# Attention and top-1 experts on one core: six products behind the next branch, an alignment directive for small products, and a new order at the first border

## The chip, the cores and the metric

The kernel runs on one core of a Trainium2 chip. The metric is the device time of one execution in microseconds (us); the time shown is the median of three runs. Durations come from one execution taken by the hardware profiler.

## The reference

Attention inside blocks of 64 rows, then a mixture of eight experts of which each row uses the best one. Everything is float32.

```python
# q, k, v: (8, 8, 576, 64); chunks of 64 rows
scores = scale * q_c @ k_c.T
attn = softmax(scores)
x = (attn @ v_c) -> (4608, 512)
logits = x @ w_gate                     # (4608, 8)
expert = argmax(logits); gate = softmax(logits)[expert]
for e in range(8):
    xe = x[expert == e]
    h = maximum(xe @ w1[e], 0.0)        # w1: (512, 1024)
    out[expert == e] = gate * (h @ w2[e])   # w2: (1024, 512)
```

## The kernel before, in words

Matrix products of float32 accuracy are made as three fp32r products: each operand is split into a high part and the rest (`whi`, `wlo`; `xhi`, `xlo`; `hh`, `hl`), and high by high, high by low and low by high are summed in PSUM. Each such product is a weight load and a matmul on TensorE.

The first 165 us compute the attention in 18 groups, the gate logits and the routing, and scatter the rows of x, sorted by expert, to a table `xd` in DRAM. Slot 0 of the expert stage is woven into it: `slot_0` is a generator whose steps `filler(n)` takes one by one. Its last three steps are: three products of m=0 and three of m=1 of its last hidden block (two steps), then `finish` for both (the last step).

The expert stage is a loop over slots. A slot is 256 rows of one expert (`BLK`), two row tiles of 128, and up to 128 extra rows (`EXT`), so that an expert's remainder needs no slot of its own. How many extra rows there are is known only at run time, so every slot's code holds three forms, chosen by `kind{u}`: `form_a` (256 rows), `form_x(64)` (320 wide) and `form_x(128)` (384 wide). In TensorE's program the 128-row form of a slot stands first, then the 64-row form, then the plain one, then the code behind the join, called the merge here. With the given data 18 slots are run; slots 1, 5 and 7 take the 64-row form, slot 11 the 128-row form, the others the plain one. Slots from 14 on (`SMIN`) stand inside a further condition.

What a slot does, with the lines before the change:
- `make_xt` (L572, L574, L575): transposes of the row tiles on TensorE into PSUM, a copy to `xhi` on ScalarE, the rest `xlo` on VectorE. Slots 0 to 2 use it. Later slots get their rows turned by `spread` (16 transfers on SP's queue), `turn` (VectorE) and `make_xs`. `make_xt_x` (L605, L607, L608) does the same as `make_xt` for the extra rows, in every slot.
- `gemm1` (L616) or `gemm1_x` (L623, L624's sum): for f = 0 to 7 twelve products into one PSUM bank; ScalarE makes `hh` (L637), VectorE `hl` (L642).
- `block(f)`: `gemm2` (L694 to L696), three products of 512 columns for m=0 (bank U) and three for m=1 (bank V). `more(f)`: `gemm2_x` for the extra rows (bank K).
- `finish(u, m)`: scales a result by the gate (L715 to L721) and scatters it to the output (L722, on POOL).

In the forms `block(f-2)` runs behind `gemm1(f)`, so the loop ends with blocks 6 and 7 open; their hidden tiles (`last`, from pool `hq`, reused by every slot) are used in the merge: both m=0 parts, `finish` 0, both m=1 parts, `finish` 1. That the order is kept comes from `manual_schedule`: each engine gets its instructions in the order in which the code is written.

At each slot's f=4 a hint is given to TensorE on the branch of the next slot. TensorE's code is fetched in blocks by DMA, on a queue named "q8 instruction". `fill_up` (L1164) puts tiny products of 8 columns into the 64- and 128-row forms, with counts from `FILL`: slot 1 has 12 behind f=4 of the 64-row form; slots from 2 on have 10 at the head of the 128-row form, and 16 at the head and 23 behind f=4 of the 64-row form. Their results are never read.

Of the kernel before, what the change touches and what calls it, by code (L numbers as in the profile page):

```python
# [18 lines left out]
P = 128  # L19
# [13 lines left out]
BLK = 256  # L33
# [5 lines left out]
XW = D + 16  # L39
HB = 3  # L40
WARM = 36
FILL = {1: (0, 0, 12), 2: (10, 16, 23)}
BIG = 1.0e6


# [1 line left out]
def attn_moe_kernel(ctx: ExitStack, tc: tile.TileContext, q, k, v, wg, w, out):  # L47
# [479 lines left out]
    def wset(u):  # L527

        return 0 if u < 2 else (u + 1) % 2
# [115 lines left out]
    def gemm1(par, f, hh=None, hl=None):  # L645
        ph = bank("X", [P, BLK]) if f % 3 == 2 else bank("S", [P, BLK])
        gemm1_pe(par, f, ph)
        return gemm1_lo(ph, relu_hi(ph, hh), hl)
# [32 lines left out]
    def filler(n):  # L681
        for _ in range(n):
            next(fill, None)
            halves[0] -= 1
# [425 lines left out]
    hx = ctx.enter_context(tc.tile_pool(name="hx", bufs=HB))  # L1110
    hq = ctx.enter_context(tc.tile_pool(name="hq", bufs=1))
    filler(halves[0] - 2)
    make_xt(1, banks="QK")
    filler(3)
    def slot(u, kd, nxt):
        par = wset(u)
        py = [bank("UV"[m], [P, D]) for m in range(2)]
        if u > 1:
            spread(u + 1)
            load_w(u + 1, 2)  # L1120

        last = [[hq.tile([P, BLK], F32R, name=f"{x}{f}") for x in ("hh", "hl")] for f in (6, 7)]

        def block(f, h, ms=(0, 1)):
            for m in ms:
                gemm2(par, f, h, m, py)

        def later():

            if u == 1:  # L1130
                yield from places()
            yield from find_u(u + 3)

        def some(x, n):
            for _ in range(n):
                next(x, None)

        def form_a():
            h = []
            x = later()  # L1140
            for f in range(8):
                h.append(gemm1(par, f, *(last[f - 6] if f > 5 else ())))
                if f == 4 and u + 1 < SMAX:

                    tc.mark_branch_hint_location(f"kind{u + 1}", hint=(nxt + 1) >> 1, engines=PE)
                if f == 0 and u > 1:
                    gather_x(u + 1)
                if f == 5 and u > 1:
                    turn()
                    gather(u + 2)  # L1150
                if f < 7:
                    split_step(u, f)
                    some(x, 4 if u == 1 else 1)
                if f > 1:
                    block(f - 2, h[f - 2])

        def form_x(n):

            make_xt_x(u, n)
            pe = bank("K", [P, D])  # L1160

            def fill_up(to, k):
                for _ in range(k):
                    nc.tensor.matmul(to[:, 0:8], ones, ones[:, 0:8], start=True, stop=True)  # L1164

            few = FILL[min(u, 2)]
            fill_up(pe, few[0] if n == EXT else few[1])
            h = []
            x = later()

            def more(f):
                gemm2_x(par, f, *h[f][1], pe)

            for f in range(8):
                h.append(gemm1_x(par, f, n, *(last[f - 6] if f > 5 else ())))
                if f == 4 and u + 1 < SMAX:
                    tc.mark_branch_hint_location(f"kind{u + 1}", hint=(nxt + 1) >> 1, engines=PE)
                if f == 0 and u > 1:
                    gather_x(u + 1)
                if f == 5 and u > 1:  # L1180
                    turn()
                    gather(u + 2)
                if f < 7:
                    split_step(u, f)
                    some(x, 4 if u == 1 else 1)
                if 1 < f < 7:
                    block(f - 2, h[f - 2][0])
                    more(f - 2)
                if f == 4 and n < EXT:
                    fill_up(bank("T", [P, P]), few[2])  # L1190
            more(5)
            more(6)
            block(5, h[5][0], (0,))
            more(7)
            finish(u, 2, pe, n)
            block(5, h[5][0], (1,))

        with tc.If(kd > 0, label=f"kind{u}") as c:
            with tc.If(kd > 1) as c2:
                form_x(EXT)  # L1200
            with c2.Else():
                form_x(EXT // 2)
        with c.Else():
            form_a()

        nc.gpsimd.drain()  # L1206
        if u == 1:
            make_xt(u + 1)
        else:
            make_xs()  # L1210
        split_chunk(wset(u + 1), 5)
        for m in range(2):
            for f in (6, 7):
                block(f, last[f - 6], (m,))
            finish(u, m, py[m], on_act=m == 0)

    n_s = nc.values_load(kind[0:1, NU:NU + 1], min_val=0, max_val=SMAX)
    PE = [mybir.EngineType.PE]
    kinds = {1: nc.values_load(kind[0:1, 1:2], min_val=0, max_val=2)}
    nest = ExitStack()  # L1220
    for u in range(1, SMAX):
        if u >= SMIN:
            nest.enter_context(tc.If(n_s > u))
        kd = kinds[u]
        if u + 1 < SMAX:
            kinds[u + 1] = nc.values_load(kind[0:1, u + 1:u + 2], min_val=0, max_val=2)
        slot(u, kd, kinds.get(u + 1))
    nest.close()
    order.__exit__(None, None, None)

# [33 lines left out]
```

## Time and profile before

| | |
|---|---|
| median of three runs | 606.31 us (605.6 to 609.58) |
| the profiled execution | 606.66 us, span 604.5 us |
| mean granted TensorE clock | 0.981 |
| TensorE matmul busy | 566.5 us, 94% of the span |
| TensorE weight load busy | 496.8 us, 82% |
| VectorE busy | 443.5 us, 73% |
| ScalarE busy | 300.9 us, 50% |
| GpSimd (POOL) busy | 265.0 us, 44% |

The span runs from the first to the last instruction; the profiled execution is some 2 us longer. The times inside the trace count from the span's start. A product is listed with the time it is busy (0.39 us for 512 columns), but products are pipelined: from the start of one to the start of the next 0.23 us pass. A number in brackets at the end of a row is the idle time of the engine ahead of it, and what ended it; "issue" is time in which the engine waited for nothing that the profile shows. An engine name with a q (PEldq) is its sequencer, which reads the program, waits for semaphores, and takes branches.

### The profile page before, as it was taken

How to read it: one execution, taken by the hardware profiler on the slowest of the kernel's cores; microseconds unless marked ns; L12 is line 12 of the kernel's file. 1: busy time of each engine (PE TensorE's matmuls, PEld its weight loads, DVE VectorE, ACT ScalarE, POOL GpSimd, SP SyncE). 2: the span in 40 equal slices, each digit the busy share in tenths (PEclk: the TensorE clock that was granted, in tenths of full speed). 3: DMA queues.
4: the chain of work that ended last, by engine and by line, in shares of the span. 5: the costliest groups of instructions: out<-in, count | busy, mean ns of one | idle time of the engine just before them, and what ended most of it. 6: DMA issues, size and time to landing. Idle time of an engine off the chain costs nothing.

```text
span 604.5 us, 14989 instructions
## 1 busy us (share of the span) xinstructions
PE 566.5 (94%) x5723; PEld 496.8 (82%) x5723; DVE 443.5 (73%) x834; ACT 300.9 (50%) x563; POOL 265.0 (44%) x275
## 2 busy tenths in 40 slices
PE   7887879779989999999999999999998999999995
PEld 5666767658878989988898888998897899899894
DVE  6687969885747677876677668788655878878774
ACT  2565556664123555554455355555434555555552
POOL 3122424474645255435264436525423453654352
PEclk9898989898989999999999999999999999999999
DMA  8999898632485364256226612358622235632021
GB/s 296 367 354 348 289 333 292 220 110 108 163 286 199 123 219 111 79 176 226 58 68 216 219 43 84 109 197 299 218 87 84 60 108 176 216 96 85 20 57 37
DMA packets 59701, 103.31 MB, mean 171 GB/s; under 512 B 16240, under 2 KB 32624, under 8 KB 55984
## 3 DMA queue, kind: packets, MB, share of 16 engines
q0 software_dynamic: 20704, 60.74, 29.5%
q1 hardware_dynamic: 38864, 40.94, 21.1%
q8 instruction: 67, 1.10, 0.8%
q14 instruction: 66, 0.54, 0.3%
HBM read 121.60 MB, written 19.82 MB: 234 GB/s over the span
## 4 chain that ended last, share of the span: by engine, by line
PE 59%; DMA 19%; issue 8%; POOL 4%; DVE 4%; POOLq 3%; ACT 2%; SPq 0%; ACTq 0%; DVEq 0%
DMA out_y<-y,oid 15%; PE psS L616 11%; PE psS L623 6%; PE psL L616 3%; PE psU L696 3%; PE psV L694 3%; PE psV L695 3%; PE psU L694 3%; PE psU L695 3%; PE psV L696 3%; PE psU L286 3%; PE psS L232 3%; POOLq L1206 2%; PE psL L623 2%; POOL raw L532 2%
## 5 line engine op out<-in xcount | busy, mean ns | idle before, releaser
L77 DVE TENSOR_TENSOR wlo<-raw,whi 128x1024 fp32r<-128x1024 f32 x134 | 163.3, 1219 | 27.0 <-ACT whi L76 24.2
L76 ACT CAST whi<-raw 128x1024 fp32r<-128x1024 f32 x134 | 139.9, 1044 | 0.5 <-issue 0.5
L532 POOL DMA_INDIRECT raw<-in_w,widx x70 | 87.9, 1256 | 108.3 <-DVE wlo L77 50.7
L637 ACT ACTIVATE hh<-psS 128x256 fp32r<-128x256 f32 x110 | 42.3, 385 | 167.2 <-PE psS L616 113.7
L616 PE MATMUL psS<-xlo,whi 128*128 128x256 f32 x344 | 97.5, 283 | 2.3 <-DVE xlo L575 2.3
L616 PE MATMUL psS<-xhi,whi 128*128 128x256 f32 x344 | 97.7, 284 | 1.1 <-PE psV L696 0.9
L616 PE MATMUL psS<-xhi,wlo 128*128 128x256 f32 x344 | 97.3, 283 | 0.0
L722 POOL DMA_INDIRECT out_y<-y,oid x40 | 46.0, 1150 | 109.7 <-issue 27.3
L642 DVE SCALAR_TENSOR_TENSOR hl<-psS,hh 128x256 fp32r<-128x256 f32 x110 | 46.3, 421 | 56.5 <-ACT hh L637 33.3
L550 POOL DMA_INDIRECT xg<-xd,idx x58 | 68.0, 1173 | 21.8 <-issue 18.3
L616 PEld LDWEIGHTS psS<-xlo,whi 128*128 128x128 f32 x344 | 65.8, 191 | 5.2 <-DVE xlo L575 2.5
L616 PEld LDWEIGHTS psS<-xhi,whi 128*128 128x128 f32 x344 | 65.7, 191 | 5.2 <-issue 1.7
L616 PEld LDWEIGHTS psS<-xhi,wlo 128*128 128x128 f32 x344 | 65.7, 191 | 0.0
L694 PE MATMUL psU<-whi,hh 128*128 128x512 f32 x144 | 57.5, 399 | 1.6 <-issue 1.6
L695 PE MATMUL psU<-wlo,hh 128*128 128x512 f32 x144 | 57.1, 397 | 0.0
L694 PE MATMUL psV<-whi,hh 128*128 128x512 f32 x144 | 56.9, 395 | 0.0
L696 PE MATMUL psU<-whi,hl 128*128 128x512 f32 x144 | 56.6, 393 | 0.2
L695 PE MATMUL psV<-wlo,hh 128*128 128x512 f32 x144 | 56.7, 394 | 0.0
L696 PE MATMUL psV<-whi,hl 128*128 128x512 f32 x144 | 56.2, 391 | 0.0
L427 POOL DMA_INDIRECT xd<-xb,di x32 | 31.5, 985 | 33.4 <-issue 21.6
L84 POOL TENSOR_TENSOR wlo<-raw,whi 128x512 fp32r<-128x512 f32 x15 | 19.0, 1277 | 52.4 <-ACT whi L83 38.6
L594 DVE STREAM_TRANSPOSE y<-xg 128x1024 f32<-128x1024 f32 x16 | 33.1, 2069 | 0.9 <-issue 0.3
(247 smaller groups left out, 1192.9 us busy)
## 6 DMA issues: line engine op xcount, KB each, us to landing
kb<-in_k SPq DMA_DIRECT2D x36, 256.0 KB
qt<-in_q SPq DMA_DIRECT2D x36, 256.0 KB
vb<-in_v SPq DMA_DIRECT2D x36, 256.0 KB
xg<-xg SPq DMA_DIRECT2D x256, 32.0 KB
raw<-in_w SPq DMA_DIRECT2D x16, 256.0 KB
raw<-in_w,widx POOLq DMA_INDIRECT x70, 3.3
xg<-xd,idx POOLq DMA_INDIRECT x58, 3.6
out_y<-y,oid POOLq DMA_INDIRECT x40, 3.2
```

The source lines that it names most:

```text
L76: nc.scalar.copy(hi, src)
L77: nc.vector.tensor_tensor(lo, src, hi.bitcast(F32), ALU.subtract)
L532: nc.gpsimd.indirect_dma_start(out=raw[c][:, :], out_offset=None, in_=w, in_offset=bass.IndirectOffsetOnAxis(ap=widx[:, u, c:c + 1], axis= ...
L550: nc.gpsimd.indirect_dma_start(out=t[:, :], out_offset=None, in_=xd[0:rows, :], in_offset=bass.IndirectOffsetOnAxis(ap=place(u, h), axis=0 ...
L616: nc.tensor.matmul(ph, a, b[:, kc, 0:BLK], start=kc + i == 0, stop=kc + i == 5)
L623: nc.tensor.matmul(ph, a[par][kc][:, f * 128:(f + 1) * 128], b[:, kc, 0:BLK + n], start=kc + i == 0, stop=kc + i == 5)
L637: nc.scalar.activation(hh, ph, AF.Relu)
L642: nc.vector.scalar_tensor_tensor(hl, ph, 0.0, hh.bitcast(F32), ALU.max, ALU.subtract)
L694: nc.tensor.matmul(py, hh, wh, start=f == 0, stop=False)
L695: nc.tensor.matmul(py, hh, wl, start=False, stop=False)
L696: nc.tensor.matmul(py, hl, wh, start=False, stop=f == 7)
L722: nc.gpsimd.indirect_dma_start(out=outs[m], out_offset=bass.IndirectOffsetOnAxis(ap=oid[u % 3][0:n, m:m + 1], axis=0), in_=y, in_offset=No ...
```

## The change

The change does four things, all on TensorE's order or driven by it:

1. The tiny products go. In their place one `addr_align` directive stands behind f=4 of the 64-row form (not in the 128-row form).
2. In slots 1 to 12 the six m=1 products of blocks 6 and 7 and `finish` 1 (now called `rest`) move from the merge into the next slot's form: ahead of `gemm1` in the plain form, between the extra rows' transposes and `gemm1_x` in the others. In their place block 5, until now the last of the form, moves into the merge. In the x forms block 4 moves behind `more(5)`. From slot 13 on `rest` is run at once, and the merge keeps 18 products.
3. The hidden tiles are now a fixed list for all slots, as many as before.
4. Slot 0's last six products stand between the transposes of slot 1's two row tiles; its `finish` stands behind both.

```diff
-FILL = {1: (0, 0, 12), 2: (10, 16, 23)}
+PLACE = {1: 180, 2: 189}
+BLOCK = 256
...
     filler(halves[0] - 2)
-    make_xt(1, banks="QK")
-    filler(3)
-    def slot(u, kd, nxt):
+    make_xt(1, 0, banks="QK")
+    filler(2)
+    make_xt(1, 1, banks="QK")
+    filler(1)
+    h_of = h0[5:8] + h0[5:8] + [[hq.tile([P, BLK], F32R, name=f"{x}{f}") for x in ("hh", "hl")] for f in (6, 7)]
+
+    def rest(u, py):
+
+        for f in (6, 7):
+            gemm2(wset(u), f, h_of[f], 1, py)
+        finish(u, 1, py[1])
+
+    def slot(u, kd, nxt, left=None):
...
         def form_a():
+            if left is not None:
+                rest(u - 1, left)
             h = []
...
-                if f > 1:
+                if 1 < f < 7:
                     block(f - 2, h[f - 2])
...
             make_xt_x(u, n)
+            if left is not None:
+                rest(u - 1, left)
             pe = bank("K", [P, D])
 
-            def fill_up(to, k):
-                for _ in range(k):
-                    nc.tensor.matmul(to[:, 0:8], ones, ones[:, 0:8], start=True, stop=True)
-
-            few = FILL[min(u, 2)]
-            fill_up(pe, few[0] if n == EXT else few[1])
...
+                if 1 < f < 6:
+                    block(f - 2, h[f - 2][0])
                 if 1 < f < 7:
-                    block(f - 2, h[f - 2][0])
                     more(f - 2)
                 if f == 4 and n < EXT:
-                    fill_up(bank("T", [P, P]), few[2])
+                    nc.tensor.addr_align(BLOCK, offset=PLACE[min(u, 2)], max_nops=0)
             more(5)
+            block(4, h[4][0])
             more(6)
-            block(5, h[5][0], (0,))
             more(7)
             finish(u, 2, pe, n)
-            block(5, h[5][0], (1,))
...
         split_chunk(wset(u + 1), 5)
-        for m in range(2):
-            for f in (6, 7):
-                block(f, last[f - 6], (m,))
-            finish(u, m, py[m], on_act=m == 0)
+        block(5, h_of[5])
+        for f in (6, 7):
+            block(f, h_of[f], (0,))
+        finish(u, 0, py[0], on_act=True)
+        if u + 1 < SMIN:
+            return py
+        rest(u, py)
...
-        slot(u, kd, kinds.get(u + 1))
+        left = slot(u, kd, kinds.get(u + 1), left)
```

TensorE at the border of slots 0 and 1 (`xg_64` are slot 1's row tiles, psQ and psK their two banks, `kind` the register with the form). Before, both row tiles' transposes come first and the six products behind them:

```order
L696 MATMUL psV<-whi_7_75,hl 128x512
L572 MATMUL psQ<-ident,xg_64 128x128 x4
L572 MATMUL psK<-ident,xg_64 128x128 x4
L694 MATMUL psU<-whi_7_75,hh 128x512
L695 MATMUL psU<-wlo_7_83,hh 128x512
L696 MATMUL psU<-whi_7_75,hl 128x512
L694 MATMUL psV<-whi_7_75,hh 128x512
L695 MATMUL psV<-wlo_7_83,hh 128x512
L696 MATMUL psV<-whi_7_75,hl 128x512
L1217 TENSOR_LOAD kind
```

After it, the same place:

```order
L697 MATMUL psV<-whi_7_75,hl 128x512
L573 MATMUL psQ<-ident,xg_64 128x128 x4
L695 MATMUL psU<-whi_7_75,hh 128x512
L696 MATMUL psU<-wlo_7_83,hh 128x512
L697 MATMUL psU<-whi_7_75,hl 128x512
L695 MATMUL psV<-whi_7_75,hh 128x512
L696 MATMUL psV<-wlo_7_83,hh 128x512
L697 MATMUL psV<-whi_7_75,hl 128x512
L573 MATMUL psK<-ident,xg_64 128x128 x4
L1227 TENSOR_LOAD kind
```

The six products have passed the second group of transposes, and the loads of the form's register stand directly behind that group (line numbers are one or more higher in the changed kernel).

TensorE at the head of slot 2's 64-row form, which stands for that of every later slot (`xg_65` are the extra rows, `ones` the operand of the tiny products). Before:

```order
L695 MATMUL psV<-wlo_6_3053,hh 128x512
L696 MATMUL psV<-whi_6_3045,hl 128x512
L1199 UNCONDITIONAL_BRANCH
L605 MATMUL psT<-ident,xg_65 128x64 x4
L1164 LDWEIGHTS ones
L1164 MATMUL psK<-ones 128x8
```

After, from the same branch on:

```order
L1206 UNCONDITIONAL_BRANCH
L606 MATMUL psT<-ident,xg_65 128x64 x4
L695 MATMUL psV<-whi_7_75,hh_3110 128x512
L696 MATMUL psV<-wlo_7_83,hh_3110 128x512
L697 MATMUL psV<-whi_7_75,hl_3111 128x512
L695 MATMUL psV<-whi_7_75,hh_3112 128x512
L696 MATMUL psV<-wlo_7_83,hh_3112 128x512
L697 MATMUL psV<-whi_7_75,hl_3113 128x512
L624 MATMUL psS<-xhi,whi_0_3039 128x320
```

The tiny products have gone, and slot 1's last six products (its weights, `whi_7_75`) stand in their place.

TensorE at the end of slot 1's merge, up to slot 2's branch. Before:

```order
L696 MATMUL psU<-whi_7_75,hl_3155 128x512
L694 MATMUL psV<-whi_7_75,hh_3152 128x512
L695 MATMUL psV<-wlo_7_83,hh_3152 128x512
L696 MATMUL psV<-whi_7_75,hl_3153 128x512
L694 MATMUL psV<-whi_7_75,hh_3154 128x512
L695 MATMUL psV<-wlo_7_83,hh_3154 128x512
L696 MATMUL psV<-whi_7_75,hl_3155 128x512
L1226 TENSOR_LOAD kind
L1198 COMPARE_AND_BRANCH
L1199 COMPARE_AND_BRANCH
```

After:

```order
L697 MATMUL psV<-whi_6_74,hl 128x512
L695 MATMUL psU<-whi_7_75,hh_3110 128x512
L696 MATMUL psU<-wlo_7_83,hh_3110 128x512
L697 MATMUL psU<-whi_7_75,hl_3111 128x512
L695 MATMUL psU<-whi_7_75,hh_3112 128x512
L696 MATMUL psU<-wlo_7_83,hh_3112 128x512
L697 MATMUL psU<-whi_7_75,hl_3113 128x512
L1237 TENSOR_LOAD kind
L1205 COMPARE_AND_BRANCH
L1206 COMPARE_AND_BRANCH
```

The branch now stands directly behind the m=0 products, the m=1 products have gone behind it, and the products of block 5 (weights `whi_6_74`) stand ahead of the m=0 ones.

## Rows read from the trace of the kernel before

**Rows 1.** Windows: length, busy time of PE, PEld, DVE, ACT, POOL, then clock, DMA share, GB/s.
```profile
164.65:168.07 3.42, 1.50 (x8) 0.85 (x6) 0.11 (x1) 0.59 (x1) 2.81 (x3) 1.00 0.67 177
168.07:171.48 3.41, 3.34 (x10) 2.58 (x10) 2.19 (x7) 0.59 (x1) 1.00 (x2) 0.50 0.84 262
200.00:427.00 227.00, 226.32 (x1460) 203.49 (x1459) 169.45 (x295) 118.01 (x197) 104.52 (x84) 1.00 0.46 148
...
462.00:581.00 119.00, 119.00 (x770) 108.69 (x769) 92.07 (x148) 65.51 (x101) 58.55 (x50) 1.00 0.36 109
```

**Rows 2.** Timeline of PE, border of slots 0 and 1: start, length, instruction, [idle before].
```profile
166.56 0.75 PE L572 MATMUL psQ<-ident,xg 128*128 128x128 f32 x4 [1.15 <-DMA xg<-xd,idx]
168.14 1.13 PE L572 MATMUL psK<-ident,xg 128*128 128x128 f32 x4 [0.83 <-DMA xg<-xd,idx]
...
169.91 0.63 PE L696 MATMUL psU<-whi,hl 128*128 128x512 f32 x1
...
171.66 0.69 PE L605 MATMUL psT<-ident,xg 64*128 64x64 f32 x4
172.81 0.86 PE L623 MATMUL psS<-xhi,whi 128*128 128x320 f32 x4 [0.46 <-ACT xhi L607]
...
176.25 0.56 PE L623 MATMUL psS<-xhi,wlo 128*128 128x320 f32 x2 [0.53 <-issue]
...
177.22 0.60 PE L623 MATMUL psL<-xhi,whi 128*128 128x320 f32 x3
```

**Rows 3.** Timeline of PE, the head of slot 5, a 64-row slot.
```profile
272.14 0.55 PE L1164 MATMUL psK<-ones 128*128 128x8 bf16 x16
272.67 0.71 PE L623 MATMUL psS<-xhi,whi 128*128 128x320 f32 x3
```

**Rows 4.** Timeline of PE, slot 5 behind f=4.
```profile
287.10 0.73 PE L1164 MATMUL psT<-ones 128*128 128x8 bf16 x23
287.69 0.68 PE L623 MATMUL psL<-xhi,whi 128*128 128x320 f32 x3
```

**Rows 5.** Timeline of PE, the head of slot 11, the 128-row slot.
```profile
423.94 0.63 PE L605 MATMUL psT<-ident,xg 128*128 128x128 f32 x4
424.41 0.39 PE L1164 MATMUL psK<-ones 128*128 128x8 bf16 x10
425.30 0.62 PE L623 MATMUL psS<-xhi,whi 128*128 128x384 f32 x2 [0.50 <-ACT xhi L607]
```

**Rows 6.** Timeline of PE, the end of slot 5.
```profile
298.60 0.39 PE L710 MATMUL psK<-whi,xh 128*128 128x512 f32 x1
...
300.42 0.39 PE L695 MATMUL psU<-wlo,hh 128*128 128x512 f32 x1
300.89 0.50 PE L696 MATMUL psU<-whi,hl 128*128 128x512 f32 x1
```

**Rows 7.** Timelines of PEld and DVE, the same place.
```profile
300.89 0.19 PEld L696 LDWEIGHTS psU<-whi,hl 128*128 128x128 f32 x1 [0.51 <-DVE y L717]
...
300.36 0.48 DVE L717 TENSOR_SCALAR y<-y,gate 64x512 f32<-64x512 f32 x1
```

**Rows 8.** PE's sequencer by source line: durations min/median/max in ns, first and last start.
```profile
L1198 PEldq COMPARE_BRANCH  x17: 78/347/3254, 169.6 to 572.0; - x17
...
L1199 PEldq COMPARE_BRANCH  x8: 70/330/3680, 169.7 to 454.0; - x8
...
L1226 PEldq TENSOR_LOAD <-kind x17: 300/307/325, 169.2 to 571.5; - x17
```

**Rows 9.** DMA queues in the window 174.0 to 175.1 us: packets, MB, share.
```profile
q0 software_dynamic: 90, 0.39, 89.4%
q8 instruction: 1, 0.02, 5.6%
```

**Rows 10.** Timeline of PE, the end of slot 11.
```profile
455.80 0.39 PE L696 MATMUL psV<-whi,hl 128*128 128x512 f32 x1
457.79 0.50 PE L694 MATMUL psU<-whi,hh 128*128 128x512 f32 x1 [1.60 <-issue]
```

More of the change, by code (lines that the diff above doesn't have):

```diff
@@ L1120, in slot @@
             load_w(u + 1, 2)
-        last = [[hq.tile([P, BLK], F32R, name=f"{x}{f}") for x in ("hh", "hl")] for f in (6, 7)]
         def block(f, h, ms=(0, 1)):
@@ L1141, in form_a @@
             for f in range(8):
[L1142 to L1153, printed above, removed]
-                if f > 1:
[L1155 to L1160, printed above, removed]
-            def fill_up(to, k):
-                for _ in range(k):
-                    nc.tensor.matmul(to[:, 0:8], ones, ones[:, 0:8], start=True, stop=True)
-            few = FILL[min(u, 2)]
-            fill_up(pe, few[0] if n == EXT else few[1])
[L1168 to L1175, printed above, removed]
+                h.append(gemm1(par, f, *h_of[f]))
                 if f == 4 and u + 1 < SMAX:
@@ L1186, in form_x, with more @@
                 if 1 < f < 7:
+                    block(f - 2, h[f - 2])
+        def form_x(n):
+            make_xt_x(u, n)
+            if left is not None:
+                rest(u - 1, left)
+            pe = bank("K", [P, D])
+            h = []
+            x = later()
+            def more(f):
+                gemm2_x(par, f, *h[f][1], pe)
+            for f in range(8):
+                h.append(gemm1_x(par, f, n, *h_of[f]))
+                if f == 4 and u + 1 < SMAX:
+                    tc.mark_branch_hint_location(f"kind{u + 1}", hint=(nxt + 1) >> 1, engines=PE)
+                if f == 0 and u > 1:
+                    gather_x(u + 1)
+                if f == 5 and u > 1:
+                    turn()
+                    gather(u + 2)
+                if f < 7:
+                    split_step(u, f)
+                    some(x, 4 if u == 1 else 1)
+                if 1 < f < 6:
                     block(f - 2, h[f - 2][0])
+                if 1 < f < 7:
                     more(f - 2)
                 if f == 4 and n < EXT:
-                    fill_up(bank("T", [P, P]), few[2])
+                    nc.tensor.addr_align(BLOCK, offset=PLACE[min(u, 2)], max_nops=0)
             more(5)
+            block(4, h[4][0])
             more(6)
-            block(5, h[5][0], (0,))
             more(7)
             finish(u, 2, pe, n)
-            block(5, h[5][0], (1,))
         with tc.If(kd > 0, label=f"kind{u}") as c:
@@ L1220, in attn_moe_kernel @@
     nest = ExitStack()
+    left = None
     for u in range(1, SMAX):
```

## The prediction

> **What bounds the kernel now.** I read the windows view first, stage by stage. From 200 to 427 us TensorE is busy 226.32 of 227.00 us, from 462 to 581 us 119.00 of 119.00, both at full clock, while VectorE, the next but for TensorE's own weight loads, has 169 and 92 [rows 1]. So in the expert stage the end moves only by what TensorE is given to do and by the places where it stands still. The second view is TensorE's timeline at those places. At the border of slots 0 and 1 it has two holes, 1.15 and 0.83 us, both ended by a gather of rows; then it runs at half the clock (0.50, the 1.2 GHz level, for 3.41 us; of its six products the last four take 169.91 to 171.66, 0.44 each, where eight at full clock take 298.60 to 300.42, 0.23 each); then 0.46 us for ScalarE's xhi and 0.53 us that end in "issue" [rows 1, 2, 6]. At the head of a 64-row slot 16 tiny products stand ahead of the first gemm [rows 3], 23 more stand behind f=4 [rows 4], and the 128-row slot's head has 10 and then a wait of 0.50 us [rows 5]. At the end of a 64-row slot one weight load waits 0.51 us for VectorE's last step on the extra rows [rows 6, 7]. The sequencer's own rows (branches, register loads) come last: they price what the new order puts next to a branch [rows 8].
>
> **The change part by part.** The sum is made against the profiled execution, 606.66 us: the span of 604.5 and some 2 us around it, 0.35 above the median of 606.31. The shipped data takes the 64-row form in slots 1, 5 and 7, the 128-row form in slot 11, the plain form elsewhere; so of slots 2 to 12, in which six products now stand behind the branch, eight are plain.
>
> *Fillers gone.* Their cost is from start to start: at slot 5's head 272.14 to 272.67, 0.53 us [rows 3]; slot 7's head shows the same pattern, so 1.06 together. Behind f=4, 287.10 to 287.69, 0.59 us, twice 1.18, and slot 1's 12 at the same rate 12/23 of 0.59, 0.31 [rows 4]. The head fillers also gave ScalarE time to make xhi. In the new order the six products of the slot before (6 x 0.23 = 1.4 us) stand in that place. Slot 1, which has no head filler, needs 172.81 - 171.66 = 1.15 us from its transposes to the first gemm, 0.69 of it the transposes [rows 2]; 0.46 us are to be covered and 1.4 cover them. The six products themselves cost nothing new: they are done once before and once after. At slot 11's head both the fillers and the wait go: 424.41 to 425.30, 0.89 us [rows 5]. Bounds: all of it, or, if xhi were late all the same, the fillers alone and not the 0.50.
>
> *The directive.* No row of this trace shows an alignment directive. Below, the nearest row is a branch that falls through, 0.07 us on the sequencer [rows 8], hidden; above, a branch whose target is not there, 3.25 to 3.68 us. TensorE's queue holds work ahead of its sequencer: the first branch of the second kind runs at 169.7 and the first instruction behind it at 171.66 [rows 2, 8], so about 1.9 us of such a stall would be hidden and some 1.6 seen. I take 0, since of 17 and 8 branches the middle ones take 0.33 to 0.35 and lie under the products. Without the fillers the padding is the directive's work, so what stands behind it keeps its place in the blocks in which code is fetched.
>
> *Slot 1's start.* Row tile 1's transposes wait for their gather until 168.14, the six products do not [rows 2]. In the new order the products start when row tile 0's transposes end, about 167.0, at the full clock that this stretch has [rows 1], and end at 167.0 + 6 x 0.23 = 168.4; the transposes then take some 0.47 at full clock, as slot 11's four do [rows 5], to 168.9. The register loads and branches stay behind the transposes of row tile 1: the last load is at 169.2, the branches from 169.6 and 169.7 [rows 8], over at about 170.1. The extra rows' transposes then start near 170.3 instead of 171.66, and gemm1 near 171.5 instead of 172.81. That gain of 1.3 us runs into the hole at 176.25. There one block of code arrives on the instruction queue at about 175, through DMA engines that weights keep busy [rows 9], and nothing in the change makes it come earlier. But the 128-row form, which lies ahead of the 64-row one in TensorE's program, gives six products of block 5 to the merge, each a weight load and a matmul; the same block border therefore falls 12 instructions, or six products, later in slot 1's work: behind 24 products instead of 18. Six of them took 176.25 to 177.22, 0.16 each [rows 2]; 24 need 3.9 us, to 175.4, so f=2 begins at 176.25 instead of 177.22: -0.97. Bounds: 0, if the border stands where it did; -1.9, if the code comes earlier too (1.3 and the hole, 0.53). VectorE's two scalings of slot 0's result stay ahead of the extra rows' xlo; they wait for products that end 3 us sooner, so they are not late.
>
> *End of a slot.* Block 4 and block 5 change places with the extra rows' products. In slot 5 the extra rows' last product starts at 298.60 and VectorE ends with them at 300.84; the sixth product behind the branch's join has to wait, 300.42 to 300.89 where 0.23 is usual: 0.24 us, twice [rows 6, 7]. In the new order twelve products follow at once: from 298.83 to 301.57, and the wait stands ahead of the last, at 301.3, with nothing left to wait for. So -0.48. But the next branch now stands behind 12 products, not 18. With the wait over at 300.84, a load of 0.31 and a branch of 0.35 [rows 8] end at 301.6 to 301.9, against 301.57 for the products: a new hole of 0 to 0.6 us, taken at 0.3, twice: +0.6. A plain slot has no such wait: the twelve products last 2.7 us, the load and a branch 0.7, and I take 0 for the eight of them. Behind that branch are queued the six products, finish 1 and its scatter, then gemm1; the scatter comes no earlier or later than its products.
>
> *What stays.* At the end of slot 11 TensorE waits 1.60 us for a branch over the other forms [rows 10]; that branch still jumps as far. Slots 13 to 17 keep their order and, busy to the last 0.01 us [rows 1], their time.
>
> Sum: -0.97 - 1.06 - 1.18 - 0.31 - 0.89 - 0.48 + 0.6 = -4.3 us. From the profiled 606.66 that gives 602.4, from the median 602.0, which I predict (-0.7%).
>
> **Rivals.**
> (a) *Slower: the plain branches miss.* Six products fewer lie ahead of each branch. If its target's code is then not there when the sequencer jumps, each of eight plain slots pays 3.25 us [rows 8] less what is still queued. With the hidden tile of f=7 made only during the merge, the branch can be reached no earlier than half of the twelve products, so some 1.3 us of cover are left: 2.0 x 8 = 16, 606.3 - 4.3 + 16 = 618. It decides from a fetch later than 2.7 us after the merge's start. Against it: the hint is given at f=4, a dozen microseconds earlier, and only the jump out of slot 11's form shows such a hole. Trainium skill, "Runtime: NRT & Kernel Launch", section "Instruction fetch mechanics": a taken branch whose target lies outside the two pages held forces a fetch before execution goes on. By that rule every jump over a form would stall; the trace agrees for the longest rows alone (3254 and 3680 ns) and not for the median, 347 and 330.
> (b) *The directive misses.* 1.6 us in slots 1, 5 and 7, +4.8 in all: 606.8, no gain. For it, the same long rows; against it, that code straight ahead is next in order.
> (c) *More than forecast.* Slot 1's code comes earlier (0.9 more), no holes at the ends of slots 5 and 7 (0.6 more), and a little of the 1.60 us behind slot 11: 599.9.
> (d) *The clock falls later instead.* Slot 1's half clock cost six products 0.2 each. If it now falls during gemm1, 3.4 us at half speed cost 1.7, and f=2 is late again: 0.97 is lost, 603 to 604.
>
> **How the numbers follow.** Forecast with (d) inside its range 0.66, (a) 0.07, (b) 0.11, (c) 0.16. A measurement of this kernel tells about 1% from no change, 6.06 us; below 600.25 lies (c) and the edge of the forecast's range. Its bounds: slot 1 from 0 to -1.9, the holes from 0 to 1.2, the wait at slot 11 either way, so 600.5 to 604. With part of (b) and (c) the range is 599.7 to 605.5. Faster by over 1%: 0.19; within 1%: 0.73; slower: 0.08.
>
> **What would show it.** TensorE's timeline of the changed kernel: no tiny products; six 512-column products between the two groups of row-tile transposes of slot 1 at 0.23 us each, f=2 of slot 1 at 176.3; the first gemm of slots 5, 7 and 11 with no wait; a hole of at most 0.6 us between the twelfth product of the merge and the transposes of the next form, and none in plain slots. The branch rows should still have medians near 0.35. Holes of 2 us behind plain merges would make (a) right, holes behind f=4 (b); f=2 of slot 1 at 177 would void the largest single term but one.

## The result and the profile after

The changed kernel takes 597.94 us (median of 4 executions, 596.52 to 600.29) against 606.35 us of the kernel before (4 executions beside it): a ratio of 0.9877, 95% interval 0.9828 to 0.9926. Forecast were 602.0 us and a range of 599.7 to 605.5. Two later comparisons of the same pair gave 0.9872 (0.9824 to 0.9920) and 0.9918 (0.9888 to 0.9949). It is faster, by some 1%, and by more than the 4.3 us that the expert stage was forecast to give. The medians here are over all executions, while the ratios leave out the few that are over 1.5% slower than the fastest of their kernel, so the two can differ by some tenths of a per cent.

The page of the changed kernel, head and TensorE's line:

```profile
span 594.4 us, 14800 instructions
...
PE 557.9 (94%) x5623; PEld 490.3 (82%) x5623; DVE 444.0 (75%) x834; ACT 300.4 (51%) x563; POOL 269.5 (45%) x275
```

The span is 594.4 us instead of 604.5, 10.1 less. To see where, the two timelines are cut at two products that both kernels have: slot 0's last product ahead of slot 1's transposes, and the last product of slot 17.

| stretch (us) | before | after | difference |
|---|---|---|---|
| attention stage, to slot 0's product | 165.01 | 160.16 | -4.85 |
| expert stage, to slot 17's last product | 431.68 | 427.20 | -4.48 |
| from there to the end | 7.78 | 7.05 | -0.73 |

Nearly half of the 10.1 lies ahead of the first instruction that the change moves: up to there every engine has the same instructions in the same order. The windows view of the changed kernel (columns as in [rows 1]):

```profile
80.00:90.00 10.00, 6.96 (x204) 5.13 (x203) 7.61 (x16) 4.46 (x11) 2.22 (x3) 1.00 0.86 306
110.00:120.00 10.00, 8.37 (x189) 6.91 (x185) 9.04 (x17) 6.42 (x17) 5.36 (x5) 1.00 0.46 160
192.00:420.00 228.00, 227.81 (x1392) 204.82 (x1391) 169.71 (x297) 118.96 (x200) 107.84 (x85) 1.00 0.48 151
453.00:572.00 119.00, 119.00 (x770) 108.70 (x770) 93.13 (x149) 65.50 (x101) 57.76 (x50) 1.00 0.36 109
```

In the last two rows the expert stage is as full as before, 227.81 of 228.00 and 119.00 of 119.00 us busy, and VectorE has not come nearer to being the bound: 169.71. In the first two, ten microseconds each of the attention stage, the granted clock is 1.00; the execution profiled of before has a stretch of about 3.4 us at 0.5 near 86 and another near 113:

```profile
80.00:90.00 10.00, 7.60 (x168) 5.58 (x164) 6.62 (x13) 4.04 (x9) 2.23 (x3) 0.83 0.85 305
110.00:120.00 10.00, 7.85 (x172) 6.72 (x171) 7.26 (x15) 5.40 (x14) 4.84 (x5) 0.83 0.48 163
```

It has five such stretches ahead of 165 us, that of the changed kernel two. A third profile of the changed kernel shows the same two windows otherwise:

```profile
80.00:90.00 10.00, 7.60 (x192) 5.79 (x191) 6.77 (x14) 4.37 (x11) 2.22 (x3) 0.83 0.87 310
110.00:120.00 10.00, 7.85 (x141) 6.38 (x145) 6.51 (x15) 5.02 (x12) 4.04 (x4) 0.66 0.44 147
```

So the half-clock stretches differ between executions of one and the same kernel.

The border of slots 0 and 1 in TensorE's timeline, which answers to [rows 2]:

```profile
160.16 0.39 PE L697 MATMUL psV<-whi,hl 128*128 128x512 f32 x1
162.30 0.75 PE L573 MATMUL psQ<-ident,xg 128*128 128x128 f32 x4 [1.76 <-DMA xg<-xd,idx]
162.80 0.48 PE L695 MATMUL psU<-whi,hh 128*128 128x512 f32 x1
...
164.05 0.40 PE L697 MATMUL psV<-whi,hl 128*128 128x512 f32 x1
164.28 0.63 PE L573 MATMUL psK<-ident,xg 128*128 128x128 f32 x4
166.02 0.66 PE L606 MATMUL psT<-ident,xg 64*128 64x64 f32 x4 [1.10 <-DMA xg<-xd,idx]
167.14 0.86 PE L624 MATMUL psS<-xhi,whi 128*128 128x320 f32 x4 [0.46 <-ACT xhi L608]
...
170.18 0.75 PE L624 MATMUL psS<-xlo,whi 128*128 128x320 f32 x4
172.30 0.85 PE L624 MATMUL psL<-xhi,whi 128*128 128x320 f32 x4 [1.37 <-issue]
```

The six products (162.80 to 164.05) stand ahead of row tile 1's transposes and run at 0.23 us each, at the full clock. The first transposes still wait for a gather, 1.76 us here; the extra rows' transposes wait 1.10 us; the hole for a block of code has moved from the middle of f=1 to the start of f=2 and is 1.37 us instead of 0.53.

Slot 5's head, its f=4 and its end, slot 11's head and end, in the same view; they answer to [rows 3 to 6] and [rows 10]:

```profile
265.04 0.69 PE L606 MATMUL psT<-ident,xg 64*128 64x64 f32 x4
265.65 0.50 PE L695 MATMUL psV<-whi,hh 128*128 128x512 f32 x1
...
267.15 0.75 PE L624 MATMUL psS<-xhi,whi 128*128 128x320 f32 x4
...
281.26 0.39 PE L711 MATMUL psK<-whi,xh 128*128 128x512 f32 x1
281.49 0.60 PE L624 MATMUL psL<-xhi,whi 128*128 128x320 f32 x3
...
294.34 0.39 PE L697 MATMUL psU<-whi,hl 128*128 128x512 f32 x1
294.81 0.50 PE L695 MATMUL psV<-whi,hh 128*128 128x512 f32 x1
...
415.07 0.63 PE L606 MATMUL psT<-ident,xg 128*128 128x128 f32 x4
415.46 0.47 PE L695 MATMUL psV<-whi,hh 128*128 128x512 f32 x1
...
416.93 0.52 PE L624 MATMUL psS<-xhi,whi 128*128 128x384 f32 x2
...
447.77 0.50 PE L695 MATMUL psU<-whi,hh 128*128 128x512 f32 x1 [1.43 <-ACT xhi L600]
...
450.42 0.39 PE L697 MATMUL psU<-whi,hl 128*128 128x512 f32 x1
450.95 0.50 PE L695 MATMUL psV<-whi,hh 128*128 128x512 f32 x1
```

No tiny products are left. Six products lie between the transposes and a first gemm that waits for nothing (267.15, 416.93). The stall ahead of the sixth product is gone, and a hole of 0.24 us stands behind the twelfth (294.34 to 294.81 where 0.23 is usual). At slot 11's end the first hole is the old one, 1.43 against 1.60 us. There is a second one behind the twelfth product, at slot 12's branch; in before it is this row, which starts 1.31 us after the start of the last product (460.42):

```profile
461.73 0.35 PE L616 MATMUL psS<-xhi,whi 128*128 128x256 f32 x1 [0.93 <-PE psV L696]
```

In the changed kernel it is 0.53 us from start to start (450.42 to 450.95), so beyond the usual 0.23 the second hole is down from 1.08 to 0.30 us.

TensorE's branches by line, which answer to [rows 8]; L1198 is the directive:

```profile
L1205 PEldq COMPARE_BRANCH  x17: 78/347/2579, 165.3 to 562.6; - x17
...
L1206 PEldq COMPARE_BRANCH  x8: 70/330/3522, 165.5 to 444.2; - x8
...
L1198 PEldq COMPARE_BRANCH  x3: 196/202/212, 179.9 to 330.7; - x3
```

The medians of the branches are as before, and so is the longest one of L1206; the directive is a branch of 0.2 us on the sequencer, three times, and no product waits for it.

### The profile page after: what moved, and what is told of

It reads as the page before. It is cut to its first block, busy times and chain, and to the rows that moved or that the text cites. A ratio compares the mean times of both kernels' runs of the same rounds, so it can differ in the third digit from the quotient of the medians.

```text
span 594.4 us, 14800 instructions
## 1 busy us (share of the span) xinstructions
PE 557.9 (94%) x5623; PEld 490.3 (82%) x5623; DVE 444.0 (75%) x834; ACT 300.4 (51%) x563; POOL 269.5 (45%) x275
## 4 chain that ended last, share of the span: by engine, by line
PE 71%; DMA 13%; issue 5%; DVE 3%; ACT 2%; POOL 2%; POOLq 2%; SPq 0%; ACTq 0%; DVEq 0%
PE psS L617 15%; DMA out_y<-y,oid 10%; PE psS L624 7%; PE psL L617 4%; PE psV L695 4%; PE psU L695 4%; PE psU L696 4%; PE psV L696 4%; PE psU L697 4%; PE psV L697 4%; PE psS L233 3%; PE psL L624 3%; PE psU L287 2%; PE psT L310 2%; PE psQ L310 1%
## 5 line engine op out<-in xcount | busy, mean ns | idle before, releaser
L723 POOL DMA_INDIRECT out_y<-y,oid x40 | 48.5, 1211 | 104.1 <-ACT hh L638 25.9
```

The lines of the kernel that those rows point to most:

```text
L723: nc.gpsimd.indirect_dma_start(out=outs[m], out_offset=bass.IndirectOffsetOnAxis(ap=oid[u % 3][0:n, m:m + 1], axis=0), in_=y, in_offset=No ...
```

## The experiments

**Is the attention stage's gain the change's?** Both kernels again, unedited, with more executions.

> The kernel before, unchanged. Theory A (the attention stage's time is the execution's own): the last product ahead of slot 1's transposes, at 165.0 us in the profile of before and 160.2 in that of the changed kernel, falls anywhere from 160 to 165 us in a new profile, the number of half-clock stretches there goes with it (5 in one, 2 in the other, about 1.7 us each), and single times spread over 4 to 5 us. Theory B (the change, through the program's length or place, makes the attention stage shorter): it is again within 0.7 us of 165.0, with five half-clock stretches ahead of it, and the median is 606 to 607 us.

> The changed kernel, unchanged. Theory A: the last product ahead of slot 1's transposes falls anywhere from 160 to 165 us; from there to the last product of slot 17 it is 427.2 us within 0.7, as in the first profile, against 431.7 before. Theory B: it is within 0.7 us of 160.2 again, and the median is 596 to 598 us, 9 us below the kernel before.

Slot 0's last product stands at 169.2 us in the kernel before and at 170.9 in the changed one; half-clock stretches number five and six ahead of it. Both lie outside the 160 to 165 us of theory A, and 4.2 and 10.7 us from where theory B put them. Over all profiles of this study it stands anywhere from 159.3 to 171.3 us: 165.0, 169.2, 171.3, 166.0 and 169.1 with the attention stage of kernels made from before, 160.2, 170.9, 170.5, 170.1, 166.1, 160.8, 165.1, 159.3 and 165.8 with kernels made from the changed one. The means, 168.1 and 165.4, are no further apart than such scatter makes them. Part of the scatter goes with the session and its chip: the four profiles of the session of these two runs lie at 169.2 to 171.3 us with no difference between the kernels, four of the next at 159.3 to 166.0, four of the last at 165.8 to 170.5. So theory A holds in its reason, with a wider spread than it said, and theory B as stated is refuted; that the change shortens the attention stage by a microsecond or two is not excluded. The medians of the timed runs were 610.96 and 602.96 us.

The expert stage, on the other hand, repeats to hundredths. Taken from one slot's first gemm to the next slot's, slots 2 to 10 and 12 to 17 of before differ by at most 0.03 us between its two profiles. Slot 11 is an exception: in the second it is 0.56 us shorter, and over the four profiles with before's POOL program it varies by 0.9 us. Against before, the changed kernel's slots differ so, in its first, second and third profile:

| slot | 4 (to slot 5's gemm) | 5 | 6 (to 7's) | 7 | 10 (to 11's) | 11 | 12 |
|---|---|---|---|---|---|---|---|
| after | -0.40 | -0.80 | -0.37 | -0.79 | -0.87 | -0.90 | -0.07 |
| second | -0.40 | -0.70 | -0.40 | -0.79 | -0.87 | +0.65 | -0.07 |
| third | -0.40 | -0.71 | -0.40 | -0.82 | -0.87 | -0.30 | -0.07 |

Slots 2, 3, 8, 9 and 13 to 17 are within 0.03 of before's. In the second profile slot 11 has a half-clock stretch at its end; in the others its first hole, 1.43 and 1.71 us, varies as it does in before (1.60 and 1.24). Slot 1 is better taken from row tile 0's transposes to slot 2's first gemm, since the gather ahead of them takes what it takes: 37.3 and 37.1 us before, 36.5, 36.2 and 36.35 after.

> The changed kernel once more, beside runs of the kernel before on the same chip. Expert stage and end together are 5.0 + 0.9 us shorter in every profile so far; if the attention stage is the same but for chance, the medians differ by 5 to 7.5 us and the slots take the same times again to 0.05 us. If the change shortens the attention stage as well, they differ by 8 or more.

The third comparison gave 604.73 against 610.97 us, 6.2 less, with the slots as in the table. The expectation's 5.0 + 0.9 us is more than the rows give: over all pairs of the two profiles of before and the three of the changed kernel the two stretches together are 4.5 to 5.8 us shorter.

**The order at the first border alone, and undone.**

```diff
# before_border_new: before with          # after_border_old: the reverse
-    make_xt(1, banks="QK")
-    filler(3)
+    make_xt(1, 0, banks="QK")
+    filler(2)
+    make_xt(1, 1, banks="QK")
+    filler(1)
```

> The kernel before with only the new order at the border of slots 0 and 1. By the prediction f=2 of slot 1 starts about 0 to 1 us earlier than before (the code border stands where it stood, so the hole at it grows by what is gained ahead of it): 12.2 us from slot 0's last product ahead of the transposes, within 0.4. From there to the end nothing changes against before: the total is that of the kernel before within 1 us of its median, unless the attention stage differs.

> The changed kernel with the old order at the border of slots 0 and 1 (both row tiles' transposes ahead of slot 0's last six products). If the new order is worth what the prediction gave it, the stretch from the last product ahead of the transposes to f=2 of slot 1 is 1 us longer than in the changed kernel (12.1) and again has a half-clock stretch. If the code fetch sets that place, as the first comparison of the traces suggests (12.2 us before, 12.1 after), it is the same within 0.4 us.

From row tile 0's transposes to f=2 of slot 1: 10.7 and 10.4 us in before, 9.8 with the new order alone, 10.0, 9.5 and 9.9 in the changed kernel, 9.8 in the changed kernel with the old order. So the new order brings nothing to the changed kernel, and 0.6 to 0.9 us to the kernel before in one execution.

The first gemm does stand nearer to those transposes with the new order: 4.2 to 4.8 us in its eight profiles, against 6.0 to 6.25 in four with the old order. But that is the clock: those four have a half-clock stretch at the border. Two profiles with the old order (the six products alone and POOL's longer program, both below) have none there, and their first gemm stands at 4.75 and 4.66 us. This is the latter:

```profile
170.44 0.75 PE L572 MATMUL psQ<-ident,xg 128*128 128x128 f32 x4 [0.94 <-DMA xg<-xd,idx]
...
175.10 0.85 PE L623 MATMUL psS<-xhi,whi 128*128 128x320 f32 x4 [0.46 <-ACT xhi L607]
...
180.24 0.89 PE L623 MATMUL psS<-xhi,wlo 128*128 128x320 f32 x2 [2.23 <-issue]
```

What is gained ahead of the code is lost at it, 2.23 us here and 1.37 in the changed kernel. The packet on the instruction queue for this code starts 7.0 to 7.7 us behind row tile 0's transposes in twelve of the thirteen profiles with no hint on slot 1's branch, whatever the order, and at 6.4 us in the thirteenth, the kernel before with the new order. Its gain goes with that one early packet, and whether the order brought it is not shown. In four of the eight profiles with the new order the half-clock stretch falls into gemm1 instead; whether the order keeps it away from the border is not shown either.

The totals tell no more: 610.61 us for the first kernel against 610.35, and 605.17 for the second, between before and the changed kernel. The first kernel's expert stage is 433.7 us, 2.0 above before's and not the same as expected: slot 8, which the edit does not touch, is 1.69 us longer in this execution, where products wait up to 0.55 us for VectorE's `hl`. Why VectorE was late there is open.

**The tiny products and the directive.** First both taken away from the kernel before.

```diff
-FILL = {1: (0, 0, 12), 2: (10, 16, 23)}
+FILL = {1: (0, 0, 0), 2: (0, 0, 0)}
```

> The kernel before with no tiny products and no directive; the order is the old one. Measured from slot 0's last product ahead of slot 1's transposes to the last product of slot 17 (431.7 and 432.0 us in two profiles of before). Theory A, the tiny products cost only their own time: the 23 and 12 behind f=4 go (-1.5), at the heads of the three wider slots from 2 on the wait for xhi takes their place (-0.2 at most): 430.2. Theory B, they keep the code at its place in the blocks that are fetched, and without them branches and code run into fetches: over 432, with branch rows of 2 to 3.7 us beyond the two that before has.

The stage takes 431.85 us, as before's and as neither theory has it. Slots 5 and 7 gain 0.68 and 0.70 (f=4), the heads nothing (the wait for xhi takes the place of the tiny products), slot 1 nothing, and slot 15 loses 1.42, where a branch takes 3.71 us that is not among before's long ones. A small part of theory B shows. The timed runs, 606.54 us against 603.90 of the kernel before (ratio 1.0034, 0.9983 to 1.0085), show no difference.

```diff
-                if f == 4 and n < EXT:
-                    nc.tensor.addr_align(BLOCK, offset=PLACE[min(u, 2)], max_nops=0)
```

> The changed kernel without the directive and with nothing in its place. The same stretch is 427.2 and 427.9 us in two profiles of the changed kernel. Theory A (the directive only replaces the tiny products and is itself free and needless): 427.5 within 0.5. Theory B (the place of the code counts, the directive keeps it): 429 to 445, holes of 1 to 2 us at branches that have none now.

Theory B, at full size: 438.01 us, 10.8 above the changed kernel, and in timed runs 609.54 us against 603.90 of the kernel before (ratio 1.0129, 1.0041 to 1.0216): without the directive the change is a loss. Slot 4 alone is 6.1 us longer than in the changed kernel, slot 1 some 4. TensorE's timeline at slot 5's head, and the second branch by line:

```profile
268.08 0.39 PE L697 MATMUL psU<-whi,hl 128*128 128x512 f32 x1
273.31 0.71 PE L606 MATMUL psT<-ident,xg 64*128 64x64 f32 x4 [4.85 <-issue]
```

```profile
L1204 PEldq COMPARE_BRANCH  x8: 70/346/5958, 164.7 to 454.1; - x8
```

A branch of 5.96 us, a hole of 4.85, and after it 3.4 us at half the clock. Trainium skill, "Runtime: NRT & Kernel Launch", section "Instruction fetch mechanics", says that a taken branch whose target is outside the pages held has to fetch; the trace agrees for the two new long branches, 3.6 us (slot 1's end) and 6.0 us (above), and shows that most branches (median 0.35) do not stall.

```diff
-PLACE = {1: 180, 2: 189}
+PLACE = {1: 180, 2: 125}
```

> The changed kernel with the directive's place moved by 64 instructions (189 to 125) in slots from 2 on. Theory A, the place matters and 189 is a chosen one: branches into or out of the 64-row form's neighbours run into fetches, the expert stage is 1 to 10 us longer than the changed kernel's 427.2 (slot 1 apart). Theory B, any fixed place will do, since every slot then has the same one: 427.2 within 0.7.

Slots 5 and 7 are 4.0 and 3.0 us longer than in the changed kernel, each behind its jump from the 64-row form to the merge; the others are as there, but for slot 11. The stage takes 432.7 us, in one execution. The first product of slot 5's merge, and the second branch by line:

```profile
299.05 0.50 PE L695 MATMUL psU<-whi,hh 128*128 128x512 f32 x1 [2.45 <-ACT xhi L600]
```

```profile
L1206 PEldq COMPARE_BRANCH  x8: 75/424/3987, 170.2 to 455.7; - x8
```

Two branches more of this line are long, 3.99 and 3.77 us, and so are those into the slots behind them, 2.73 and 3.05 us. Of slot 5's 4.0 us a part is a half-clock stretch right behind the hole. So what counts is the place, not that it is fixed.

```diff
                 if f == 4 and n < EXT:
+                    t = bank("T", [P, P])
+                    for _ in range(12 if u == 1 else 23):
+                        nc.tensor.matmul(t[:, 0:8], ones, ones[:, 0:8], start=True, stop=True)
                     nc.tensor.addr_align(BLOCK, offset=PLACE[min(u, 2)], max_nops=0)
```

> The changed kernel with the 12 or 23 tiny products put back ahead of the directive in the 64-row form; the code behind the directive keeps its place. By the prediction's term for them the stretch is 1.5 us longer than in the changed kernel: 428.7 to 429.4. If they were hidden, it is the same as there.

428.57 us, 1.4 more than the first profile of the changed kernel: 0.66 and 0.65 in slots 5 and 7 and 0.2 in slot 1. The term holds. In timed runs the ratio to before is 0.9940 (0.9897 to 0.9982).

**The six products alone.** As the last edit, with the tiny products at the heads (10 and 16) and the old border order too.

> The changed kernel with the tiny products put back at the heads and behind f=4 and with the old order at the first border: what is left of the change is the six products behind the next branch (and the directive). The tiny products cost 1.5 + 1.06 + 0.39 here, so if the terms of the prediction add up the stretch is 427.5 + 2.95 = 430.4, 1.4 below before: the wait at slot 11's head, the stall ahead of the sixth product twice, less the new holes, and the end of slot 11. If the six products alone bring nothing, it is 431.7 to 432.

432.20 us, above both figures, but with a half-clock stretch in slot 1, which is 2.5 us longer than the changed kernel's there. Without slot 1 the slots sum to 1.1 us less than before's: +0.02, +0.23, +0.01 and +0.04 in slots 4 to 7, -0.60 and -0.72 in slots 10 and 11. So at the ends of slots 5 and 7 the move loses 0.3 us in all; what it brings is slot 11's head, 0.60. The 0.72 in slot 11 are its second hole, for which POOL's program, longer here too, is a candidate (below). The directive's branch runs once here, in slot 1, and not three times: in slots 5 and 7 the tiny products alone put the code at the place that the directive asks for. In timed runs the ratio to before is 0.9961 (0.9910 to 1.0011).

**Where the end gained 0.7 to 1.2 us.** From the last product to the end it is 7.78, 8.06, 7.95 and 8.08 us in the four profiles with before's POOL program (the expectation below counts one too many), 6.56 to 7.20 in the nine with the changed one, which is 86 instructions longer (the moved `finish` stands in three forms).

```diff
             make_xt_x(u, n)
+            if u == SMAX - 1 and n == EXT:
+                for _ in range(86):
+                    nc.gpsimd.drain()
```

> The kernel before with 86 instructions added to POOL's program in a branch that is never taken (the 128-row form of the last slot), as many as the change adds to POOL. From the last product to the end it is 7.8 to 8.1 us in five profiles with before's POOL program and 6.9 to 7.2 in seven with the changed one. Theory A (the end waits for a block of POOL's code, and the place of POOL's last instructions in their block decides): 6.9 to 7.3. Theory B (another part of the change shortens the end): 7.8 to 8.1.

7.19 us, in one execution: theory A. POOL's branch that ends the slots and its last drains by line, in before, in the changed kernel and in this one (name, times, min/median/max in ns, first and last start):

```profile
L1228 POOLq COMPARE_BRANCH  x6: 38/44/50, 510.9 to 601.8; - x6
L1260 POOLq DRAIN  x3: 46/111/306, 603.3 to 604.2; - x3
```

```profile
L1239 POOLq COMPARE_BRANCH  x6: 38/44/50, 501.4 to 592.8; - x6
L1271 POOLq DRAIN  x3: 46/107/210, 593.0 to 594.1; - x3
```

```profile
L1231 POOLq COMPARE_BRANCH  x6: 38/44/50, 515.5 to 606.8; - x6
L1263 POOLq DRAIN  x3: 46/107/210, 607.0 to 608.1; - x3
```

The first drain starts 6.6 us behind the last product in before (596.69), 5.6 in the changed kernel (587.36) and 5.8 here (601.22). From the start of the last branch to it 1.5 us pass in before and 0.2 in the other two; over all profiles POOL stands still behind that branch for 1.0 to 1.5 us in the four with before's POOL program and for 0.12 to 0.13 in the ten others. From 601.2 to 603.4 us of before one packet alone moves, on an instruction queue (q14, 8 KB, at 601.7). The added instructions are never run; only the place of those behind them has changed. The same run has slot 11 1.12 us shorter than before: slot 12's branch over the wider forms takes 2.53 us there, 2.50 to 2.94 in every kernel with the changed POOL program and 3.10 to 3.45 in the four without. That points at POOL's program for slot 11's second hole too, with one run. How it would reach a fetch of TensorE was not found.

**A version that is faster.** The hole ahead of slot 1's f=2 remains, and slot 1's branch is the only one without a hint.

```diff
     filler(halves[0] - 2)
+    n_s = nc.values_load(kind[0:1, NU:NU + 1], min_val=0, max_val=SMAX)
+    PE = [mybir.EngineType.PE]
+    kinds = {1: nc.values_load(kind[0:1, 1:2], min_val=0, max_val=2)}
+    tc.mark_branch_hint_location("kind1", hint=(kinds[1] + 1) >> 1, engines=PE)
     make_xt(1, 0, banks="QK")
...
-    n_s = nc.values_load(kind[0:1, NU:NU + 1], min_val=0, max_val=SMAX)
-    PE = [mybir.EngineType.PE]
-    kinds = {1: nc.values_load(kind[0:1, 1:2], min_val=0, max_val=2)}
     nest = ExitStack()
```

> The changed kernel with the first branch's hint: the loads of the form's registers and a hint for slot 1's branch stand ahead of the row tiles' transposes. In the changed kernel f=2 of slot 1 waits 1.37 us for a block of code whose fetch starts 4 us behind the branch. Theory A (the hint brings that code early): no hole ahead of f=2, and slot 2's first gemm stands 1 to 1.5 us nearer to the first row tile's transposes than in the changed kernel (36.3 us there); the total 1 to 1.5 us below the changed kernel. Theory B (the late block is the one behind the branch's target, which the hint does not fetch): the hole stays, within 0.3 us.

TensorE's timeline at its border:

```profile
168.42 0.75 PE L573 MATMUL psQ<-ident,xg 128*128 128x128 f32 x4 [1.94 <-DMA xg<-xd,idx]
...
170.40 0.63 PE L573 MATMUL psK<-ident,xg 128*128 128x128 f32 x4
171.42 0.66 PE L606 MATMUL psT<-ident,xg 64*128 64x64 f32 x4 [0.39 <-issue]
172.62 0.85 PE L624 MATMUL psS<-xhi,whi 128*128 128x320 f32 x4 [0.53 <-ACT xhi L608]
...
176.07 0.75 PE L624 MATMUL psS<-xlo,whi 128*128 128x320 f32 x4
176.66 0.75 PE L624 MATMUL psL<-xhi,whi 128*128 128x320 f32 x4
```

The hole is gone (176.07 to 176.66 without a break), and the extra rows' transposes wait 0.39 us instead of 1.10. The packet of code starts 5.3 us behind row tile 0's transposes instead of 7.0 to 7.7, and slot 1's branches run at 2.0 instead of 2.8 to 3.2 us. The edit moves the register loads forward as well as giving the hint; which of the two does it is not separated. From row tile 0's transposes to slot 2's gemm it is 34.5 us instead of 36.2 to 36.5; slot 2 gives 0.67 back at a branch. The expert stage takes 426.0 us. In timed runs: 603.34 against 604.73 us of the changed kernel in the same session, ratios to before of 0.9888 (0.9855 to 0.9921) and 0.9918 (0.9888 to 0.9949), so the trace shows the gain and the timing does not yet separate it.

## Why the prediction was wrong

The sign was right, and most of the mechanism; the time fell below the range.

*The range.* The failing step is "The sum is made against the profiled execution", carried on into "600.5 to 604": it took the attention stage as the same in every execution. The runs showed in its place a stage that ends anywhere from 159.3 to 171.3 us, and 4.85 us earlier in the profile of the changed kernel than in that of before; the three times of before already spread over 4 us. The interval of the first ratio reaches 3 us either way, which no term of the expert stage covers. Of the 8.4 us, 5.2 are found in the expert stage and at the end (4.5 to 5.8 over all pairs of profiles); the rest lies in the attention stage, where no instruction was changed and where the later pairs, 7.4 and 6.2 us apart, leave less. How much of it is chance is not shown; by the third ratio, 0.9918, the changed kernel would stand at 601.4 us beside the 606.35 of the kernel before, inside the range.

*The terms.* "-0.97" for slot 1's start and "0.31" for its tiny products: 0.6 to 1.1 us together where 1.28 was forecast. The hole moved to f=2 as reckoned, by block 5's six products, and the code came no earlier: "nothing in the change makes it come earlier" held. The new border order, by which the text brings gemm1 forward by 1.3 us, has no part in it: with the old one f=2 stands at 9.8 us behind row tile 0's transposes, with the new at 9.5 to 10.0. "1.06" for the heads: 0.8, since a first product behind transposes costs 0.11 more than one behind a product (265.65 to 265.99). "1.18" behind f=4: 1.3. "0.89" at slot 11's head: 0.87. "The directive ... I take 0": right, 0.2 us hidden. "-0.48" and "+0.6" at the ends of slots 5 and 7, +0.1 together: -0.2 to -0.3 in the changed kernel, +0.3 in that with the six products alone; the holes are 0.24 where 0.3 was taken. In all, these terms come to 3.8 to 4.4 us, where 4.3 was forecast.

There the text also miscounts: the merge had 12 products ahead of the next branch before as well, six of them others. Rival (a) was argued from six fewer and fell with it. And nine plain slots, not eight, now have six products behind their branch, since slot 13 runs those of slot 12.

*Two terms put at nothing.* Under "What stays" only the first hole at slot 11's end is named, and "that branch still jumps as far" held: it is 1.2 to 1.8 us with before's program and 1.2 to 1.9 with the changed one. The second, at slot 12's branch, has no term; it went from 0.9 to 1.3 us in the four profiles with before's POOL program to 0.2 to 0.6 in those with the changed one that have no half-clock stretch there. The end of the kernel, 0.7 to 1.2, was no term either. Both come with POOL's longer program, as far as one run shows, which the sum never looked at.

*The rivals.* (a) and (b) did not happen as forecast; but the runs without the directive and with it 64 instructions off show that branches can wait for code at such places, for 10.8 us in all and for 7.0 us in two slots. (c) came nearest, 599.9, but mostly not for its reasons: slot 1's code came no earlier and the 1.60 us behind slot 11 stayed; only the ends of slots 5 and 7 brought 0.3 to 0.4 of its 0.6. (d) occurs in some executions (at 178 us in the third profile) and not in others, and costs little: f=2 stands at 9.9 us there against 10.0 and 9.5 without it, since f=2 waits for its code anyway.

## What to carry to other kernels

Cut both timelines at instructions that the change cannot have touched before any term is compared, and put the spread of what lies ahead of them into the range. Where a program branches over code of some hundred instructions, treat the place of each target in its fetch block as a quantity of its own: padding that costs nothing to run decided over 10.8 us here when it was left out and over 7.0 when it was moved, and its right value was not to be seen from what the removed padding cost.

## What the runs showed of the hardware

Most slots of the expert stage repeat to 0.03 us from execution to execution. Slot 11, with its two long branches, varies by 0.9 us, and one slot 8 was 1.69 us longer. The attention stage, with the DMA engines up to 0.87 busy, scatters over 12 us between all profiles and over 2 to 7 us within a session, and carries two to six stretches of 3.4 to 10 us at half the clock (0.5, the 1.2 GHz level). Instructions that are never executed shifted the end of the kernel by 0.6 to 0.9 us, in one run. Of the 350 rows of the two form branches on TensorE's sequencer in the fourteen profiles, 69 take under 0.1 us, 229 take 0.3 to 0.5, 35 take 2.5 to 6.0, and 17 lie between.
